# One scan per unit over all 128 rows, with small transfers for the fourth pair of heads

## The chip, the cores and the metric

The kernel runs on one core of one Trainium2 chip. The metric is the device time of one execution in microseconds. The kernel before takes 502.21 us (median of three runs, 501.99 to 503.38). A profiled execution of its own gives the rows that are quoted here; a line number such as L550 is a line of the kernel before.

## The reference

A linear attention with a decaying state is followed by a two-layer network with a piecewise gate. There are 4 batches, 8 heads, 768 steps and 48 channels per head, all in float32:

```
state = zeros(B, H, D, D)
for t in range(S):
    cur    = outer(u * k[t], v[t])
    y[t]   = r[t] @ (state + cur)
    state  = w[t][:, None] * state + outer(k[t], v[t])
x = y as (B*S, 384)
h = x @ w_in                                  # 384 -> 2048
g = h where h >= 1, 0 where h <= -1, else (h + 1)**2 / 4
out = g @ w_out                               # 2048 -> 384
```

w lies between 0.8 and 0.95, so products of w over 64 steps stay within float32.

## The kernel before, in words

**Units and blocks.** Time is cut into 12 units (0 to 11) of 64 steps for all 4 batches, 256 tokens each (`UT`). Two units make one block of 512 tokens; the network works on 6 blocks. For each block and each of 16 slices f of the hidden layer there is a step: nine products in (L1348), the gate on ScalarE and VectorE, nine products out (L1368). The last three blocks are "fast": their products out are combined in a scheme with fewer multiplications (L1042), for which sums of weight parts are built first (L964, `sums_of`). Each 32-bit number is carried as a high and a low part of the reduced type fp32r.

**One attention unit** (`attention(u, ...)`). Channels stand in the rows: a head has 48 channels and takes 64 rows, 16 of them padding, so two heads fill 128 rows and the 8 heads make 4 pairs. Two pairs are one half q, so w comes as two tiles of 520 columns (2 pairs x 4 batches x 65) and r and k as two tiles of 2 x 512. VectorE scans each half forward (L550: running products of w, called p) and backward (L545, called y), multiplies k by y (L571) and r by p (L621). The last p of each chunk is the chunk's total decay; ScalarE copies it to `ptot`. Then TensorE does:

- `among` (L591), 64 small products of scaled k with scaled r, whose lower triangle VectorE picks into `r_` (L597);
- `ktrans` (L630), transposes of k; `umat` (L660), k by v, the addition to the state;
- `cross` and `along` (L703), r with the old state and the picked matrix with v.

VectorE adds to the state and multiplies it by the total decay (`step` L678, `fade` L681, reading `ptot`). ScalarE and VectorE bring the result into the block's x, and six small transfers per unit put the result's fourth pair from the tile `last` into the 16 padding rows of the three other pairs (`fill`, L827). From unit 6 on, ScalarE checks w against 1 on the loaded tile (`guard`, L846 and L847); w of the units before is loaded again for this in the fast stage. Units 0 to 2 (`early`) get the term with u by a second `among`; later units get it from POOL and VectorE on the natural layout `nk`. Units 0 and 1 are `alone`: their x gets the fourth pair through TensorE (L800).

**Buffers.** w and r/k have three tiles for halves each, so one and a half units fit. In the fast stage the attention's tiles are used again: the gate's results lie in r/k tiles 0 to 2, and the sums of weights are built in the p tile (`part`).

**The order of the work.** `Plan` takes each operation with its engine, an assumed cost, what it reads and writes, and a due time, and simulates the engines. Each engine takes the ready operation with the smallest key. The result is one fixed order per engine, written out by hand, and semaphores keep the engines together. The first keys come from due times (`LEADS`, `group`); then 40 rounds draw new keys from the latest possible times plus noise from `SEED`, and the order with the earliest simulated end is kept. For a transfer it takes 0.63 or 0.45 us on SP's queue, then bytes at 390 KB per us plus 2.0 us, and 0.15 us until the reader can go; at most eight are in flight. Where TensorE would be idle early on, products of zeros are filled in (L439). If a check finds w or the running products out of bounds, a general kernel runs afterwards; it is not touched by the change.

Of the kernel before, what the change touches and what calls it, by code (L numbers as in the profile page):

```python
# [23 lines left out]
UT = 256  # L24
# [5 lines left out]
SEG = 2 * NC * (C + 1)  # L30
HP = 64
# [17 lines left out]
SCRATCH = 2048  # L49
# [9 lines left out]
BACK, SHAKES, SHAKE, SEED = 4, 40, 0.7, 1  # L59
# [278 lines left out]

GUARDED = 6
# [17 lines left out]
def attention_moe(tc, a):  # L357
# [24 lines left out]
    seeds = one([128, 2 * NC, C + 1], F32, "seeds")  # L382
# [4 lines left out]
    wq = tiles(3, [128, SEG + 1], F32, "wq")  # L387
    rk = tiles(3, [128, 2, 512], F32, "rk")
# [3 lines left out]
    p_ = one([128, 4 * NC, C + 1], F32, "p")  # L392
    y_ = one([128, SEG], F32, "y")
# [29 lines left out]
    for t, v, name in ((zero, 0.0, "zero"), (seeds, 0.0, "seeds"), (minus_one, -1.0, "minus_one")):  # L423
        op("POOL", 0.5, SOON, (), [name], lambda t=t, v=v: G.memset(t, v))
# [79 lines left out]

    def attention(u, when, lead=None):
# [12 lines left out]
        slot = [(2 * u + 1 - q) % 3 for q in range(2)]  # L518
        pv = p_.rearrange("p (q n) c -> p q n c", q=2)
# [6 lines left out]
        for q in (1, 0):  # L526
            load(due, wq[slot[q]], a["w"][u, q], [("w", slot[q])], first=rank(1 - q))
            load(due, rk[slot[q]], a["rk"][u, q], [("k", slot[q]), ("r", slot[q])], first=rank(4 - 2 * q))
# [10 lines left out]
        sv = seeds.rearrange("p n c -> p (n c)")  # L539

        def scan(q, back):
            w = wq[slot[q]]
            if back:
                V.reciprocal(seeds[:, :, C], pv[:, q, :, C])
                V.tensor_tensor_scan(  # L545
                    out=y_[:, ::-1], data0=w[:, SEG:0:-1], data1=sv[:, ::-1], initial=0.0, op0=ALU.mult, op1=ALU.add
                )
            else:
                V.memset(seeds[:, :, C], 0.0)
                V.tensor_tensor_scan(  # L550
                    out=pv[:, q].rearrange("p n c -> p (n c)"), data0=w[:, 0:SEG], data1=sv, initial=0.0,
                    op0=ALU.mult, op1=ALU.add,
                )

        def parts(q, i):
            return rk[slot[q]][:, i].rearrange("p (n c) -> p n c", c=C)

        def with_u(q):
            for pr in range(2):
                cs = slice(pr * UT, pr * UT + UT)  # L560
                A.mul(ku[:, q, cs], rk[slot[q]][:, 1, cs], u_col[:, 2 * q + pr : 2 * q + pr + 1])

        for q in (1, 0):
            s = slot[q]
            if early:
                op("ACT", 1.0, due, [("k", s), "cst"], [("ku", q), "nk"], lambda q=q: with_u(q))
            op("DVE", 1.3, due, [("w", s)], [("p", q), "seeds"], lambda q=q: scan(q, False), port=True)
            op("ACT", 0.2, due, [("p", q)], [("ptot", u, q)], lambda q=q: A.copy(
                ptot[:, 16 * u + 8 * q : 16 * u + 8 * q + 8], pv[:, q, :, C]))
            op("DVE", 1.45, due, [("w", s), ("p", q)], ["y", "seeds"], lambda q=q: scan(q, True), port=True)  # L570
            op("DVE", 0.69, due, ["y"], [("k", s)], lambda q=q: V.tensor_tensor(  # L571
                out=parts(q, 1), in0=parts(q, 1), in1=y_.rearrange("p (n c) -> p n c", c=C + 1)[:, :, 1:], op=ALU.mult), port=True)

        def tokens(q, i, pr, c2, g=None):
            lo = pr * UT + c2 * 128 + (0 if g is None else g * C)
            return slice(lo, lo + (128 if g is None else C))


        dv = d_.rearrange("p c (a h) -> p h a c", h=2)

        def among(to, left):

            for pair in range(4):
                q, pr = divmod(pair, 2)
                for c2 in range(2):
                    for g in range(2):
                        for h in range(2):
                            i = slice(HP * h, HP * h + HP)
                            cs = tokens(q, 0, pr, c2, g)
                            lo = (pair * 2 + c2) * C  # L590
                            PE.matmul(  # L591
                                bank[to[h]][HP * g : HP * g + C, lo : lo + C], lhsT=left(q)[i, cs],
                                rhs=rk[slot[q]][i, 0, cs], start=True, stop=True,
                            )
# [6 lines left out]
        both = [("r", slot[0]), ("r", slot[1])]  # L601
        if early:
            bd = [take(), take()]
            op("PE", 1.27, due, [("ku", 0), ("ku", 1), "nk", *both], [("b", bd[0]), ("b", bd[1])],
               lambda: among(bd, lambda q: ku[:, q]), code=128)
# [14 lines left out]
        for q in (1, 0):  # L620
            op("DVE", 0.69, due, [("p", q)], [("r", slot[q])], lambda q=q: V.tensor_tensor(  # L621
                out=parts(q, 0), in0=parts(q, 0), in1=pv[:, q, :, 0:C], op=ALU.mult), port=True)
# [3 lines left out]
        def ktrans(q, b):  # L626
            for pr in range(2):
                for c2 in range(2):
                    lo = (pr * 2 + c2) * 128
                    PE.transpose(out=bank[b][:, lo : lo + 128], in_=rk[slot[q]][:, 1, tokens(q, 1, pr, c2)], identity=ident)  # L630

        op("PE", 1.27, due, [("k", slot[0]), ("k", slot[1]), *both], [("b", ba[0]), ("b", ba[1])],
# [805 lines left out]
```

## Time and profile before

| what | value |
|---|---|
| profiled execution | 502.04 us, span 500.5 us |
| median of three runs | 502.21 us |
| TensorE (PE) busy | 486.8 us, 97% |
| VectorE (DVE) busy | 402.8 us, 80% |
| ScalarE (ACT) busy | 314.3 us, 63% |
| GpSimd (POOL) busy | 102.5 us, 20% |
| moved by DMA | 54.3 MB, mean 108 GB/s |
| granted TensorE clock | 0.992 |

The span is the time from the first to the last instruction; the execution's own time is 1.5 us longer. A share of busy time is a mean over stages with different limits, so the table alone does not say what bounds the kernel. In a timeline row the columns are start, length, engine, line, operation, tiles and count, all times in us. In a group's row there are count, busy time, mean length in ns, the engine's idle time just before, and what ended that idle time.

### The profile page before, as it was taken

How to read it: one execution, taken by the hardware profiler on the slowest of the kernel's cores; microseconds unless marked ns; L12 is line 12 of the kernel's file. 1: busy time of each engine (PE TensorE's matmuls, PEld its weight loads, DVE VectorE, ACT ScalarE, POOL GpSimd, SP SyncE). 2: the span in 40 equal slices, each digit the busy share in tenths (PEclk: the TensorE clock that was granted, in tenths of full speed). 3: DMA queues.
4: the chain of work that ended last, by engine and by line, in shares of the span. 5: the costliest groups of instructions: out<-in, count | busy, mean ns of one | idle time of the engine just before them, and what ended most of it. 6: DMA issues, size and time to landing. Idle time of an engine off the chain costs nothing.

```text
span 500.5 us, 13728 instructions
## 1 busy us (share of the span) xinstructions
PE 486.8 (97%) x5767; PEld 426.3 (85%) x5767; DVE 402.8 (80%) x702; ACT 314.3 (63%) x658; POOL 102.5 (20%) x80
## 2 busy tenths in 40 slices
PE   6989999999999999999999999999999999999994
PEld 4679988889999998887878878889898989899884
DVE  6999999997787898898979988787877575675563
ACT  4769988936455566655645746778876565465451
POOL 1745515403111121112032132432200000000000
PEclk9989999999999999999999999999999999999998
DMA  8987641424242434436256012122241000100002
GB/s 316 357 331 265 251 151 64 138 45 155 74 155 85 140 124 134 160 121 225 44 203 201 11 53 85 31 62 44 42 107 22 0 2 1 53 12 0 3 1 69
DMA packets 33286, 54.30 MB, mean 108 GB/s; under 512 B 15424, under 2 KB 22720, under 8 KB 33216
## 3 DMA queue, kind: packets, MB, share of 16 engines
q1 hardware_dynamic: 32784, 52.95, 31.8%
q8 instruction: 47, 0.77, 0.7%
q10 hardware_dynamic: 432, 0.39, 0.2%
q14 instruction: 23, 0.19, 0.1%
HBM read 47.04 MB, written 4.72 MB: 103 GB/s over the span
## 4 chain that ended last, share of the span: by engine, by line
PE 92%; DVE 4%; issue 2%; DMA 1%; ACT 1%; SPq 0%; DVEq 0%; ACTq 0%
PE h L1348 41%; PE acc L1368 21%; PE acc L1042 10%; PE bank L1042 9%; PE bank L703 4%; PE bank L591 3%; PE bank L630 2%; PE bank L660 1%; DVE fl L487 1%; DMA cst<-in_consts 1%; DVE y L545 1%; DVE r L597 0%; DVE rk L571 0%; PE h L660 0%; DVE wt L490 0%
## 5 line engine op out<-in xcount | busy, mean ns | idle before, releaser
L1348 PE MATMUL h<-x,wt 128*128 128x512 f32 (+1 forms) x1035 | 221.4, 362 | 2.2 <-DVE x L779 1.4
L1348 PEld LDWEIGHTS h<-x,wt 128*128 128x128 f32 x1035 | 169.7, 190 | 30.9 <-DVE x L779 1.6
L1368 PE MATMUL acc<-gh,wt 128*128 128x256 f32 (+1 forms) x402 | 80.0, 334 | 0.0
L1368 PEld LDWEIGHTS acc<-gh,wt 128*128 128x128 f32 x402 | 61.3, 188 | 7.8
L1004 DVE SCALAR_TENSOR_TENSOR rk<-rk,h 128x512 f32<-128x512 f32 x48 | 32.8, 684 | 36.3 <-ACT rk L1003 36.0
L1157 ACT ACTIVATE g<-h 128x256 f32<-128x256 f32 (+1 forms) x67 | 31.8, 475 | 46.5 <-PE h L1348 41.4
L1001 ACT ACTIVATE rk<-h 128x512 f32<-128x512 f32 x48 | 28.7, 597 | 42.8 <-PE h L1348 42.7
L485 POOL TENSOR_SCALAR wraw<-fl 128x768 uint16<-128x768 f32 x13 | 41.5, 3195 | 47.2 <-ACT wraw L483 46.2
L1159 DVE SCALAR_TENSOR_TENSOR g<-g,h 128x256 f32<-128x256 f32 (+1 forms) x67 | 35.2, 528 | 12.6 <-ACT g L1158 11.2
L1368 PE MATMUL acc<-gl,wt 128*128 128x256 f32 (+1 forms) x201 | 44.5, 329 | 0.0
L1161 ACT CAST gh<-g 128x256 fp32r<-128x256 f32 (+1 forms) x67 | 32.9, 498 | 13.4 <-DVE g L1159 7.9
L617 POOL TENSOR_TENSOR r<-cst,d 128x512 f32<-128x512 f32 x18 | 21.6, 1222 | 90.2 <-PE bank L703 46.8
L1162 DVE TENSOR_TENSOR gl<-g,gh 128x256 fp32r<-128x256 f32 (+1 forms) x67 | 39.0, 591 | 1.0 <-ACT gh L1161 0.6
L1368 PEld LDWEIGHTS acc<-gl,wt 128*128 128x128 f32 x201 | 32.4, 188 | 4.0
L1158 ACT ACTIVATE g<-g 128x256 f32<-128x256 f32 (+1 forms) x67 | 33.9, 511 | 1.0
L550 DVE TENSOR_TENSOR_SCAN p<-wq,seeds 128x520 f32<-128x520 f32 x24 | 30.8, 1284 | 3.1 <-DMA wq<-in_w 2.2
L609 POOL TENSOR_TENSOR nk<-nk 128x768 f32<-128x768 f32 x9 | 17.4, 1933 | 71.8 <-DMA nk<-in_nk 49.4
L545 DVE TENSOR_TENSOR_SCAN y<-wq,seeds 128x520 f32<-128x520 f32 x24 | 30.4, 1266 | 0.8
L1003 ACT ACTIVATE rk<-rk 128x512 f32<-128x512 f32 x48 | 30.4, 633 | 0.9
L1010 DVE TENSOR_TENSOR gl<-rk,gh 128x512 fp32r<-128x512 f32 x36 | 25.8, 720 | 4.1 <-ACT gh L1009 3.9
L1010 DVE TENSOR_TENSOR g_again<-rk,nk_again 128x512 fp32r<-128x512 f32 x33 | 23.3, 710 | 6.8 <-ACT nk_again L1009 6.5
L1009 ACT CAST gh<-rk 128x512 fp32r<-128x512 f32 x36 | 22.1, 616 | 8.3 <-DVE rk L1004 5.7
(214 smaller groups left out, 910.8 us busy)
## 6 DMA issues: line engine op xcount, KB each, us to landing
rk<-in_rk SPq DMA_DIRECT2D x24, 512.0 KB, 5.4
wraw<-in_wbits SPq DMA_DIRECT2D x16, 768.0 KB, 6.9
nk<-in_nk SPq DMA_DIRECT2D x9, 768.0 KB, 5.6
wq<-in_w SPq DMA_DIRECT2D x24, 260.5 KB, 3.4
vn<-in_v SPq DMA_DIRECT2D x12, 384.0 KB, 7.0
last<-in_w SPq DMA_DIRECT2D x12, 256.0 KB, 2.9
out_y<-xf SPq DMA_DIRECT2D x15, 128.0 KB, 1.8
out_y<-g SPq DMA_DIRECT2D x6, 256.0 KB, 2.2
```

The costliest lines, as they stand in the source:

```text
L485: op(on, 0.62 if f in SIGNS else 3.2, due, [("fl", k)], [("raw", f)], lambda: e.tensor_scalar(out=half(1), in0=s, scalar1=0.0, scalar2=327 ...
L545: V.tensor_tensor_scan(out=y_[:, ::-1], data0=w[:, SEG:0:-1], data1=sv[:, ::-1], initial=0.0, op0=ALU.mult, op1=ALU.add)
L1004: op("DVE", 0.66, due, [("h", n)], [qk], lambda: V.scalar_tensor_tensor(out=gf, in0=gf, scalar=1.0, in1=bank[plan.given[hk]], op0=ALU.min, ...
L1010: op("DVE", 0.67, due, [key, ("h", i, k)], fresh_in(("l", i, k)), lambda: V.tensor_tensor(out=spare(k, 3 + i), in0=x, in1=spare(k, i).bitc ...
L1042: PE.matmul(bank[i][:, half * UT : half * UT + UT], lhsT=w[wi], rhs=g[gi], start=(b, i) not in opened, stop=True, skip_group_check=True)
L1157: op("ACT", c, due, [("h", n)], [("g", gk)], lambda: nc.scalar.activation(gs, hs(), AF.Relu, scale=0.5, bias=0.5), uses=[hk])
L1158: op("ACT", c, due, (), [("g", gk)], lambda: nc.scalar.activation(gs, gs, AF.Square))
L1159: op("DVE", 0.13 + 0.53 * k, due, [("h", n)], [("g", gk)], lambda: nc.vector.scalar_tensor_tensor(out=gs, in0=gs, scalar=1.0, in1=hs(), op ...
L1161: op("ACT", c, due, [("g", gk)], [("gh", gk)], lambda: nc.scalar.copy(ghs, gs))
L1162: op("DVE", 0.17 + 0.54 * k, due, [("g", gk), ("gh", gk)], [("gl", gk)], lambda: nc.vector.tensor_tensor(out=gls, in0=gs, in1=ghs.bitcast( ...
L1348: nc.tensor.matmul(hp, lhsT=wx[f][:, cs], rhs=xt[:, j, :], start=n == 0, stop=n == 8)
L1368: nc.tensor.matmul(o[j], lhsT=wx[f][:, cs], rhs=gt, start=first and i == 0, stop=stop and i == 2, skip_group_check=True)
```

## The change

**Dense rows.** From unit 2 on (the third unit), w, r and k come in a dense layout of three slots of 4 x 64 steps: slots are the pairs 0, 1 and 2 in their own rows, and the 48 channels of pair 3's two heads lie in the 16 padding rows of each half, a third in each slot. One forward and one backward scan over 780 columns (`LONG`) replace two of 520; one product with y and one with p do for the unit. Then `gather` sends pair 3's scaled k, and in the same way r, to the rows of its own: six transfers of 16 KB each for k and six for r, from tile to tile, issued by SP.

**In place.** In units 3 to 11 r is multiplied by p before the backward scan, which then writes over p. Unit 2 writes y into the tile `xf[0]`, takes pair 3 of the unscaled k and r from two extra loads (for its product with u), and gathers over them.

**Padded units.** Units 0 and 1 keep two halves. Their w and scans lie in `xf`, and r and k are loaded separately.

**The total decay.** r gets a 65th column of ones per chunk, so its product with p leaves the total there; `fade` and `step` read it instead of `ptot`. `ptot` is still copied for the check, and `ptot` and `above` are filled by POOL first, as not all their columns are written.

**TensorE.** `among` and `inter` read 48 rows per head instead of 64.

**Buffers.** w: two tiles for whole units. r and k: two tiles for whole units. `y` is gone and p is smaller. In the fast stage the gate's results lie in the first 1024 columns of both r/k tiles, differences in the last 1024 columns of the first, and the sums of weights are built in the last 1024 columns of the second. The guard runs once per unit over 780 columns. `SCRATCH` is 1024 instead of 2048 and `SEED` 8 instead of 1.

```diff
-SCRATCH = 2048
+SCRATCH = 1024
-BACK, SHAKES, SHAKE, SEED = 4, 40, 0.7, 1
+BACK, SHAKES, SHAKE, SEED = 4, 40, 0.7, 8
+PADDED = {0, 1}
...
-    wq = tiles(3, [128, SEG + 1], F32, "wq")
-    rk = tiles(3, [128, 2, 512], F32, "rk")
+    wd = one([128, 2, LONG + 1], F32, "wd")
+    rk = tiles(2, [128, 4 * NC * (C + 1) + 4 * UT], F32, "rk")
...
+        if padded:
+            for q in (1, 0):
+                load(due, flat_of(xf[0])[:, q * (SEG + 1) : (q + 1) * (SEG + 1)], a["w"][u, q], [("xw", q)], first=rank(1 - q))
+                load(due, rt_[:, 2 * q : 2 * q + 2]..., a["rq"][u, q], keys("r", 2 * q, 2 * q + 1), first=rank(4 - 2 * q))
+                load(due, kd_[:, 2 * q : 2 * q + 2]..., a["kq"][u, q], keys("k", 2 * q, 2 * q + 1), first=rank(4 - 2 * q))
+        else:
+            load(due, wd[:, buf], a["wd"][u], [("w", buf)])
+            load(due, kd_[:, 0:3].rearrange("p a t -> p (a t)"), a["kd"][u], keys("k", 0, 1, 2))
+            load(due, rt_[:, 0:3].rearrange("p a n c -> p (a n c)"), a["rd"][u], keys("r", 0, 1, 2))
...
+        def gather(of, t, size):
+            for j in range(3):
+                for h in range(2):
+                    lo = HP * h
+                    op("SP", 0.63, due, [(of, buf, j)], [(of, buf, 3, j, h)], lambda t=t, j=j, lo=lo: nc.sync.dma_start(
+                        out=t[lo + 16 * j : lo + 16 * j + 16, 3], in_=t[lo + D : lo + HP, j]), size=16 * 4 * size)
...
+            op("DVE", cp, due, [wk], [pk, "seeds"], lambda w=w, p=p, n=n: scan(w, p, None, n), port=True)
+            if in_place:
+                scaled_r(pairs, p, pk, cr)
+                gather("r", rt_.rearrange("p a n c -> p a (n c)"), NC * (C + 1))
+            op("DVE", cy, due, [wk, pk], [yk, "seeds"] + ..., lambda w=w, p=p, y=y, n=n: scan(w, p, y, n), port=True)
+            op("DVE", ck, due, [yk], keys("k", *pairs), lambda pairs=pairs, y=y: times_y(pairs, y), port=True)
+            if not padded:
+                gather("k", kd_, UT)
...
-            return ptot[:, 16 * u : 16 * u + 16].rearrange("p (a c g) -> p c g a", c=2, g=2)[:, :, g]...
+            return rt_.rearrange("p a (c g) t -> p c g a t", g=2)[:, :, g, :, C]...
...
-        for q in range(2):
-            if u >= GUARDED:
-                guard(wq[slot[q]][:, 0:SEG], ("w", slot[q]), 2 * u + q, (when, 0.0))
+        if u >= GUARDED:
+            guard(wd[:, buf, 0:LONG], ("w", buf), 2 * u, (when, 0.0), 1.5)
...
-    quad = [quads(mem(("q", k), flat(rk[k], 0, 1024), ("k", k), ("r", k))) for k in range(2)]
-    diff = quads(mem("t", flat(rk[2], 0, 1024), ("k", 2), ("r", 2)))
+    quad = [quads(mem(("q", k), rk[k][:, 0:1024], *rk_keys[k])) for k in range(2)]
+    diff = quads(mem("t", rk[0][:, 1024:2048], *rk_keys[0]))
...
-    part = flat(p_, 0, 1024)
-    mem("a", None, ("p", 0), ("p", 1))
+    part = rk[1][:, 1024:2048]
+    mem("a", None, *rk_keys[1])
```

More of the change, by code (lines that the diff above doesn't have):

```diff
@@ L422, in attention_moe @@
     SOON = 0, 200.0
-    for t, v, name in ((zero, 0.0, "zero"), (seeds, 0.0, "seeds"), (minus_one, -1.0, "minus_one")):
+    for t, v, name in ((zero, 0.0, "zero"), (seeds, 0.0, "seeds"), (minus_one, -1.0, "minus_one"), (ptot, 1.0, "ptot"), (above, 0.0, "above")):
         op("POOL", 0.5, SOON, (), [name], lambda t=t, v=v: G.memset(t, v))
@@ L516, in vs, with keys @@
             return v[i, c2, head * D : head * D + n]
-        slot = [(2 * u + 1 - q) % 3 for q in range(2)]
-        pv = p_.rearrange("p (q n) c -> p q n c", q=2)
+        buf = u % 2
+        padded = u in PADDED
+        in_place = not early
+        rt_, kd_ = rt[buf], kd[buf]
+        late_key = [(j, h) for j in range(3) for h in range(2)]
+        def keys(of, *pairs):
+            out = []
+            for pair in pairs or range(4):
+                out += [(of, buf, pair)] if pair < 3 else [(of, buf, 3, *x) for x in late_key]
+            return out
+        rkeys, kkeys = keys("r"), keys("k")
         ku = nk.rearrange("p a b c -> p (a b c)")[:, 0:1024].rearrange("p (q c) -> p q c", q=2)
@@ L555, in parts @@
-        def parts(q, i):
-            return rk[slot[q]][:, i].rearrange("p (n c) -> p n c", c=C)
-        def with_u(q):
[L559 to L572, printed above, removed]
@@ new lines, in attention, with scaled_r @@
+        if early:
+            for q in (1, 0):
+                op("ACT", 1.0, due, [*keys("k", 2 * q, 2 * q + 1), "cst"], [("ku", q), "nk"], lambda q=q: with_u(q))
+        def scaled_r(pairs, p, pk, cost):
+            op("DVE", cost, due, [pk], keys("r", *pairs), lambda: times_p(pairs, p), port=True)
+        for q, pairs, w, wk, p, pk, y, yk, (cp, cy, ck, cr) in todo:
+            n = len(pairs) * NC
+            op("DVE", cp, due, [wk], [pk, "seeds"], lambda w=w, p=p, n=n: scan(w, p, None, n), port=True)
+            lo = 16 * u + 8 * q
+            op("ACT", 0.2, due, [pk], [("ptot", u, q), "ptot"], lambda p=p, n=n, lo=lo: A.copy(ptot[:, lo : lo + n], by_chunk(p, n)[:, :, C]))
+            if in_place:
+                scaled_r(pairs, p, pk, cr)
+                gather("r", rt_.rearrange("p a n c -> p a (n c)"), NC * (C + 1))
+            op("DVE", cy, due, [wk, pk], [yk, "seeds"] + ([("xw", 1)] if not padded and not in_place else []), lambda w=w, p=p, y=y, n=n: scan(w, p, y, n), port=True)
+            op("DVE", ck, due, [yk], keys("k", *pairs), lambda pairs=pairs, y=y: times_y(pairs, y), port=True)
+            if not padded:
+                gather("k", kd_, UT)
@@ L619, in attention @@
                     in1=dv[:, h].unsqueeze(3).broadcast_to([128, 4, 2, C]), op=ALU.mult), port=True)
-        for q in (1, 0):
-            op("DVE", 0.69, due, [("p", q)], [("r", slot[q])], lambda q=q: V.tensor_tensor(
-                out=parts(q, 0), in0=parts(q, 0), in1=pv[:, q, :, 0:C], op=ALU.mult), port=True)
+        if not in_place:
+            for _, pairs, _, _, p, pk, _, _, costs in todo:
+                scaled_r(pairs, p, pk, costs[3])
+            if not padded:
+                gather("r", rt_.rearrange("p a n c -> p a (n c)"), NC * (C + 1))
         ba = [take(), take()]
@@ L1216, in attention_moe @@
             products(n)
-    every = [("ptot", u, q) for u in range(NU) for q in range(2)] + [("above", n) for n in range(2 * NU)]
+    every = ["ptot", "above"] + [("ptot", u, q) for u in range(NU) for q in range(2)] + [("above", n) for n in range(2 * NU)]
     op("DVE", 1.0, (len(steps) - 12, 0.0), (), [*every, "ok"], check)
```

126 lines of the change are left out of this document (76 added, 50 removed).

## The prediction

> **What bounds the kernel now.** I read the busy time in stages first, because a mean over the whole run mixes a start, a long middle and an end with different limits. Columns: stage, its length, then busy time and count for PE, weight loads, DVE, ACT and POOL, then granted clock, DMA share and GB/s.
>
> ```profile
> 0.00:40.00 40.00, 33.23 (x672) 26.00 (x675) 34.06 (x50) 25.28 (x47) 20.31 (x20) 0.96 0.84 314
> 40.00:60.00 20.00, 19.63 (x260) 19.26 (x251) 19.07 (x35) 18.76 (x44) 9.43 (x4) 1.00 0.74 268
> 60.00:300.00 240.00, 239.72 (x3506) 206.59 (x3505) 213.16 (x367) 145.86 (x332) 54.40 (x33) 1.00 0.37 124
> 300.00:484.00 184.00, 184.00 (x1270) 164.84 (x1270) 129.42 (x240) 120.44 (x231) 18.39 (x24) 1.00 0.13 32
> 484.00:500.50 16.50, 10.19 (x78) 9.57 (x76) 7.05 (x14) 3.99 (x7) 0.00 (x0) 0.87 0.17 53
> ```
>
> From 60 to 484 us TensorE is busy 423.72 of 424 us at the full granted clock. VectorE is at 89% (213.16 of 240) in the stage that holds most attention units and at 70% in the one after. So VectorE is busy there without being the limit. Only the first 40 us (DMA at 0.84, DVE at 34 of 40) and the last 16 us leave TensorE short of work, and part of its 33.23 us in the start is filler on the zero tile. The list of TensorE's waits says the same; its first rows are:
>
> ```profile
> PE h L445 <- POOL zero L424: 2.8, 1, 2.8
> PE h L1348 <- DVE x L779: 1.4, 1, 1.4
> ```
>
> 2.8 us is the wait for the first memset, and no group of later waits reaches 1.5 us. Nothing that VectorE does after 60 us is waited for in a way that could be won back.
>
> **What is removed: VectorE work.** These groups (instructions, busy us, mean ns) are the work whose shape changes. 24 scans of each kind are 12 units with two halves each.
>
> ```profile
> L550 DVE TENSOR_TENSOR_SCAN p<-wq,seeds 128x520 f32<-128x520 f32 x24 | 30.8, 1284 | 3.1 <-DMA wq<-in_w 2.2
> L545 DVE TENSOR_TENSOR_SCAN y<-wq,seeds 128x520 f32<-128x520 f32 x24 | 30.4, 1266 | 0.8
> L621 DVE TENSOR_TENSOR rk<-rk,p 128x512 f32<-128x512 f32 x24 | 17.3, 726 | 0.0
> L571 DVE TENSOR_TENSOR rk<-rk,y 128x512 f32<-128x512 f32 x24 | 16.7, 697 | 4.9 <-DMA rk<-in_rk 4.8
> L847 ACT ACTIVATE wq<-wq,minus_one 128x520 f32<-128x520 f32 x12 | 8.8, 732 | 0.2
> L846 ACT ACTIVATE wq<-wq 128x520 f32<-128x520 f32 x12 | 7.7, 639 | 6.6 <-DVE y L545 6.6
> ```
>
> A dense unit scans 780 columns once instead of 520 twice. In proportion to columns the forward scan is 1.284 x 780/520 = 1.93 us instead of 2.57, the backward one 1.90 instead of 2.53, the product with k (768 columns) 1.05 instead of 1.39, and the product with r (780) 1.11 instead of 1.45. That is 0.64 + 0.63 + 0.34 + 0.34 = 2.0 us per unit, 20 us over the ten dense units (2 to 11, counted from 0). ScalarE's guards save 2 x (0.732 + 0.639) - 1.5 x (0.732 + 0.639) = 0.69 us in each of six units. For units 3 to 11 all of this lies beside a full TensorE, since unit 3's first scan is this one:
>
> ```profile
> 75.77 1.24 DVE L550 TENSOR_TENSOR_SCAN p<-wq,seeds 128x520 f32<-128x520 f32 x1
> ```
>
> Priced at zero, with a gain of at most the 0.28 us that TensorE is short of 240 as the other end. Loaded bytes fall too (two w of 260.5 KB and two rk of 512 KB become 390, 384 and 390 KB; unit 2 adds 258 KB), where the DMA share is 0.37: zero again. The TensorE products keep count and columns, but 48 instead of 64 rows go in. The nearest rows are products of the same 64 columns with 48 and with 64 on the other side of the tile:
>
> ```profile
> L703 PE MATMUL bank<-r,vn 64*48 64x64 f32 x128 | 2.2, 217 | 0.0
> L703 PE MATMUL bank<-r,vn 64*64 64x64 f32 x640 | 11.1, 218 | 0.0
> ```
>
> One nanosecond apart: zero, with both ends there. VectorE's fade now reads the total beside r, in the same shape: zero.
>
> **The start.** Only unit 2's dense work can touch the part where TensorE is not full. In VectorE's timeline its forward scan stands right ahead of a weight's decode, and the chain that ended last runs through that decode.
>
> ```profile
> 36.84 1.24 DVE L550 TENSOR_TENSOR_SCAN p<-wq,seeds 128x520 f32<-128x520 f32 x1
> 38.00 1.51 DVE L487 SCALAR_TENSOR_TENSOR fl<-fl,wraw 128x768 int32<-128x768 int32 x1
> ```
>
> If the new order moves the scan behind the decode, 1.24 us is gained; if it stays as one 1.86 us scan, 0.62 us is lost. I take the middle, **-0.3 us**.
>
> Units 0 and 1 keep their padded halves, but r and k come as two transfers per half. SP's issues take 0.43 us each, and two more stand ahead of the first weight (first row; the others are used below):
>
> ```profile
> 3.31 0.43 SPq L469 DMA_DIRECT2D wraw<-in_wbits  x1
> 8.31 0.33 SPq L419 DMA_DIRECT2D rk<-in_rk  x1
> 18.48 0.33 SPq L419 DMA_DIRECT2D wq<-in_w  x1
> 18.91 1.95 SPq L419 DMA_DIRECT2D rk<-in_rk  x2
> ```
>
> Ends 0 and +0.9 us; I take 0, since the bytes ahead of it are the same and the DMA engines are 84% busy over these 40 us, so the weight waits for bytes and not for its issue. Unit 1's w must now wait in SP's order until unit 0 has scanned (its two staging places are single). In the chain, unit 0's last scan and unit 1's first one are
>
> ```profile
> 8.94 1.25 DVE y L545
> 15.49 1.25 DVE p L550
> ```
>
> so that wait ends 5.3 us (15.49 - 10.19) before the data is used. The two memsets of ptot and above join POOL's first ones; they read zero because the filler needs only the zero tile.
>
> **What is added: 12 small transfers per unit.** The scaled r and k of the fourth pair go back to their own rows, six SP issues of 16 KB each, and the first `among` of scaled k waits for the last. The nearest thing in the trace is the spread of `last` into x: the same partition-to-partition kind, six at a time, 16 or 32 KB (KB, then median us to landing), and over all 60 of them the least, median and most:
>
> ```profile
> x<-last SPq DMA_DIRECT2D x36, 32.0 KB, 2.9
> xf<-last SPq DMA_DIRECT2D x24, 16.0 KB, 3.5
> DMA to landing us min/median/max: 1.7/2.9/6.6
> ```
>
> The planner writes one fixed order per engine. For such a transfer it reckons 2.04 us from issue to landing and 0.15 us for the signal: 2.19 us. The time that the plan knows costs nothing, since it starts the unit earlier and fills TensorE with products meanwhile. What it does not know is 2.9 - 2.19 = 0.71 us, or 3.5 - 2.19 = 1.31 us by the 16 KB row. TensorE stops for that only if the plan put `among` closer than this behind its last input, because its queue is in order and every product behind it waits too. How close it puts them now: VectorE's last product of a unit, and the `among` in the chain that ended last.
>
> ```profile
> 171.85 0.68 DVE L621 TENSOR_TENSOR rk<-rk,p 128x512 f32<-128x512 f32 x1
> 255.25 0.68 DVE L621 TENSOR_TENSOR rk<-rk,p 128x512 f32<-128x512 f32 x1
> 272.53 1.55 DVE L621 TENSOR_TENSOR rk<-rk,p 128x512 f32<-128x512 f32 x1
> 294.77 0.68 DVE L621 TENSOR_TENSOR rk<-rk,p 128x512 f32<-128x512 f32 x1
> ```
>
> ```profile
> 173.50 1.09 PE bank L591 x64
> 255.98 1.16 PE bank L591 x64
> 274.72 1.09 PE bank L591 x64
> 296.73 1.09 PE bank L591 x64
> ```
>
> The distances are 0.97, 0.05, 0.64 and 1.28 us for units 5, 9, 10 and 11. At 0.71 us late the stops are 0.66 + 0.07 = 0.7 us; at 1.31 us they are 0.34 + 1.26 + 0.67 + 0.03 = 2.3 us; units not listed count as zero. I take **+0.7 us**, by the median of all 60, with 0 and +2.3 us as ends. Behind the waiting issues on SP stand the next loads; with two whole buffers for w, r and k now, they have a unit's time to spare (18.7 and 22.0 us between the last three rows above).
>
> The Trainium skill speaks against such transfers: "DMA: Bandwidth & Descriptors", section Rules for kernel authors, says to coalesce, since under 64 KB one mostly pays overhead; its section Anatomy of one DMA puts that overhead at about 2.0 us. The spread's 2.9 us median is longer than that page's figure; by 2.0 us the plan would be right, no stop would follow, and the sum would be 0.7 us lower.
>
> **Sum.** The profiled run is 502.04 us (span 500.5). 502.04 - 0.3 + 0.7 = 502.4; the median of the runs is 0.17 us above the profiled one, so 502.6 us.
>
> **Rivals.** (1) Late transfers decide, slower. Place: the `among` of scaled k in units 2 to 11. It decides once a transfer lands over 2.19 us plus the unit's distance after its issue. At the 16 KB row's 3.5 us that is +2.3 us over the units listed: 502.21 + 2.3 = 504.5; at longer landings (6.6 us occurs) up to 507. For it: distances as small as 0.05 us. Against: the plan may keep more distance now that the buffers are double.
>
> (2) The fast stage's sums start late, slower. They were written over p, which was free once VectorE had multiplied r in the last unit; now they share the last unit's r and k buffer, which TensorE reads until the end of `along`.
>
> ```profile
> 295.97 0.75 DVE L964 TENSOR_TENSOR p<-wt 128x256 f32<-128x256 f32 x2
> 299.79 0.68 DVE L964 TENSOR_TENSOR wq_again<-p,wq_again 128x512 fp32r<-128x512 f32 x1
> ```
>
> ```profile
> 303.03 1.56 PE bank L703 x96
> ```
>
> ```profile
> 308.00 0.30 PEld L1042 LDWEIGHTS bank<-gh,wq_again 128*128 128x128 f32 x2
> ```
>
> Now the first sums take 295.97 to 300.47, 4.5 us. If they wait for 304.59 they end at 309.1, against the first product that uses them, at 308.00: 1.1 us late, and the later pairs follow through the same buffer, so 502.21 + 1.1 = 503.3 us, and up to twice or three times that, 505. Against: `rk<-in_rk` is what VectorE waits for in L571 (4.8 us); with two whole buffers the last unit can load and run earlier.
>
> (3) The start becomes shorter, faster. SP stood until 18.48 us for a w slot and issued unit 1's second r and k behind it at 18.91 us; the new buffer is free from the beginning, so it can be issued beside the first ones, at 8.31. If that and the lighter unit 2 take away four tenths of the 6.77 us (40 - 33.23) in which TensorE stood idle in the start, 2.7 us by this estimate, the time is 502.2 - 2.7 = 499.5. Against: the DMA engines were busy anyway, and the first product waited for unit 0's x (1.4 us above), not for unit 1.
>
> The plan's seed changes too, so the whole order is drawn anew. That adds spread of either sign that no row prices.
>
> **How the numbers follow.** My forecast 0.38, rivals 0.23, 0.08 and 0.31. About 0.3% (1.5 us) is what a measurement of this kernel tells from no change. The forecast lies inside it, so same 0.38; rivals 1 and 2 give slower 0.31; rival 3 gives faster 0.31. Around 502.21, the terms' lower ends give 502.21 - 1.24 - 0.28 = 500.7 and their upper ends 502.21 + 0.62 + 0.9 + 2.3 = 506.0, the forecast's own range. With rival 3, rival 1 beyond its row and the spread of the new order, the range is 498.7 to 506.5 us.
>
> **What would show it.** Right: scans of 780 columns at 1.9 us, TensorE still full from 60 to 484 us, a TensorE wait on L591 or L630 for a DMA of about 1 us in all. Wrong upward: such waits of 2 us or more in total, or a gap in TensorE at the start of the fast stage. Wrong downward: the stage 0 to 40 us holds more products and less filler. If the scan's time did not follow its columns, the VectorE figures are wrong, but not the time.

## The result, and the profile after

The changed kernel takes 508.14 us (median of 4 runs, 506.37 to 509.55); the kernel before took 502.70 beside it (4 runs). The ratio is 1.0105, 95% interval [1.0076, 1.0135]. A second series gave 508.60 us and 1.0102 [1.0065, 1.0139]. The change makes the kernel about 1% slower, 1.6 us beyond the upper end of the predicted range. The profiled execution of after is one of 507.15 us with a span of 505.6 us.

VectorE did what was forecast. The groups of the profile after (count, busy us, mean ns, idle time ahead):

```profile
L580 DVE TENSOR_TENSOR_SCAN p<-wd,seeds 128x780 f32<-128x780 f32 x10 | 19.1, 1913 | 0.4
L583 DVE TENSOR_TENSOR_SCAN p<-wd,seeds 128x780 f32<-128x780 f32 x9 | 16.0, 1783 | 0.4
...
L598 DVE TENSOR_TENSOR rk<-rk,p 128x780 f32<-128x780 f32 x10 | 10.2, 1015 | 3.2 <-DMA rk<-in_rd 3.2
L593 DVE TENSOR_TENSOR rk<-rk,p 128x768 f32<-128x768 f32 x9 | 8.6, 951 | 0.0
```

The windows of after, by the same edges as before:

```profile
0.00:40.00 40.00, 33.41 (x692) 25.54 (x696) 33.85 (x51) 23.93 (x45) 18.83 (x21) 1.00 0.87 319
40.00:60.00 20.00, 19.85 (x243) 18.93 (x233) 19.05 (x30) 18.37 (x42) 10.66 (x3) 1.00 0.40 133
60.00:300.00 240.00, 238.16 (x3601) 205.38 (x3600) 195.06 (x309) 138.38 (x310) 57.73 (x38) 1.00 0.39 128
300.00:484.00 184.00, 184.00 (x1143) 164.52 (x1143) 128.30 (x236) 119.24 (x225) 15.97 (x20) 1.00 0.12 31
```

From 60 to 300 us VectorE fell from 213.16 to 195.06 us, and TensorE stayed full but for 1.84 us. So the added time hardly shows as idle time. It shows as more busy time for the same work: the first rows of the two pages, before and then after, have the same 5767 TensorE instructions and 4.0 us between them.

```profile
PE 486.8 (97%) x5767; PEld 426.3 (85%) x5767; DVE 402.8 (80%) x702; ACT 314.3 (63%) x658; POOL 102.5 (20%) x80
```

```profile
PE 490.8 (97%) x5767; PEld 428.5 (85%) x5767; DVE 385.9 (76%) x642; ACT 306.9 (61%) x630; POOL 103.2 (20%) x82
```

A stop of a tenth of a microsecond between two overlapping small products counts as busy, so such a loss must be looked for in the lengths of groups. In the chain that ended last (start, length, engine, tile, line, count), `among` took 1.09 us in nearly every unit before. After:

```profile
83.96 1.57 issue
...
152.28 1.09 PE bank L645 x64
...
171.95 1.33 PE bank L645 x64
...
193.96 1.33 PE bank L645 x64
...
212.52 1.38 PE bank L645 x64
...
228.98 1.38 PE bank L645 x64
```

Of these only unit 4 (152.28) is at the old length; the other four are about a quarter of a microsecond longer. The first row is a gap in the middle of unit 2's `along` in which TensorE waits for nothing that this view shows (more on it at the end). TensorE's waits name no transfer as the cause of a stop in `among`:

```profile
PE h L449 <- POOL zero L428: 3.2, 1, 3.2
PE bank L758 <- issue: 1.6, 1, 1.6
PE bank L685 <- DVE rk L593: 1.2, 2, 0.8
PE h L1401 <- DVE x L832: 0.9, 1, 0.9
PE bank L853 <- DMA nk<-in_perm: 0.6, 1, 0.6
```

And the small transfers are not late (KB each, then median us from issue to landing):

```profile
rk<-rk SPq DMA_DIRECT2D x60, 16.2 KB, 1.8
rk<-rk SPq DMA_DIRECT2D x60, 16.0 KB, 2.1
```

These are medians; the longest of the 120 took 4.8 us. Even so, in this trace the last of a unit's twelve transfers had landed 2.3 us or more before the 49th product of `among`, the first one of the fourth pair, in nine of the ten dense units. In unit 11 it had landed 0.03 us before it, and that `among` is no longer than unit 5's.

**Where the 5.1 us went.** I added up, over all TensorE products of the two profiled executions, the distance from one start to the next less a fixed length for its shape (233.3 ns for 512 columns, 116.7 for 256, 109 for the transposes, 17 for the small ones; filler on the zero tile counts as lost, and so do the time before the first product and the time after the last). What is left over is time that TensorE lost:

| stage or kind | before, us | after, us | difference |
|---|---|---|---|
| 0 to 60 us | 25.4 | 24.8 | -0.6 |
| 60 to 300: `among` | 0.04 | 1.94 | +1.9 |
| 60 to 300: products of 256 columns | 2.58 | 4.24 | +1.7 |
| 60 to 300: `cross` and `along`, with the gap of 1.57 | -0.91 | 0.95 | +1.9 |
| 60 to 300: all others | 3.1 | 3.3 | +0.2 |
| after 300 us | 8.27 | 8.33 | +0.1 |
| all | 38.5 | 43.6 | +5.1 |

Three suspects follow from this table: the waits on the small transfers, a dearer 256-column product, and the order of the work. The layout gives the second a cause to test: with the changed tiles, x, the gate's results, the state, the picked matrix `r_` and the transposed k stand 64 bytes further on, modulo 512.

### The profile page after: what moved, and what is told of

Its sections match the earlier page's. It is cut to its first block, busy times and chain, and to the rows that moved or that the text cites. A ratio compares the mean times of both kernels' runs of the same rounds, so it can differ in the third digit from the quotient of the medians.

```text
span 505.6 us, 13831 instructions
## 1 busy us (share of the span) xinstructions
PE 490.8 (97%) x5767; PEld 428.5 (85%) x5767; DVE 385.9 (76%) x642; ACT 306.9 (61%) x630; POOL 103.2 (20%) x82
## 4 chain that ended last, share of the span: by engine, by line
PE 90%; DMA 4%; DVE 2%; issue 1%; ACT 1%; SPq 1%; DVEq 0%
PE h L1401 40%; PE acc L1421 20%; PE acc L1095 10%; PE bank L1095 9%; PE bank L758 4%; PE bank L645 3%; DMA wraw<-in_wbits 2%; PE bank L685 2%; DMA rk<-in_rq 1%; PE bank L715 1%; DMA out_y<-g 1%; SPq L423 1%; DVE fl L491 0%; PE bank L443 0%; PE h L715 0%
## 5 line engine op out<-in xcount | busy, mean ns | idle before, releaser
L489 POOL TENSOR_SCALAR wraw<-fl 128x768 uint16<-128x768 f32 x13 | 43.3, 3345 | 44.5 <-ACT wraw L487 32.9
L1215 DVE TENSOR_TENSOR gl<-g,gh 128x256 fp32r<-128x256 f32 (+1 forms) x67 | 40.6, 618 | 2.3 <-ACT gh L1214 2.2
L1063 DVE TENSOR_TENSOR gl<-rk,gh 128x512 fp32r<-128x512 f32 x36 | 24.2, 685 | 2.7 <-ACT gh L1062 2.6
L1062 ACT CAST nk_again<-rk 128x512 fp32r<-128x512 f32 x33 | 20.4, 617 | 9.5 <-DVE rk L1057 6.9
L651 DVE COPY_PREDICATED r<-below,bank 128x512 f32<-128x512 int32 x23 | 16.1, 731 | 5.0 <-PE bank L645 4.9
```

What stands on the lines that cost most here:

```text
L489: op(on, 0.62 if f in SIGNS else 3.2, due, [("fl", k)], [("raw", f)], lambda: e.tensor_scalar(out=half(1), in0=s, scalar1=0.0, scalar2=327 ...
L1062: op("ACT", 0.6, due, [key], fresh_in(("h", i, k)), lambda: A.copy(spare(k, i), x))
L1063: op("DVE", 0.67, due, [key, ("h", i, k)], fresh_in(("l", i, k)), lambda: V.tensor_tensor(out=spare(k, 3 + i), in0=x, in1=spare(k, i).bitc ...
L1215: op("DVE", 0.17 + 0.54 * k, due, [("g", gk), ("gh", gk)], [("gl", gk)], lambda: nc.vector.tensor_tensor(out=gls, in0=gs, in1=ghs.bitcast( ...
```

## The experiments

All were run beside the kernel before, five rounds each.

**Are the transfers, their issues or the reads of them what costs?** Two kernels keep the changed kernel's order of work. One sends the transfers where nobody reads them, the other drops them; both leave out the fourth pair's transferred rows.

```diff
-                        out=t[lo + 16 * j : lo + 16 * j + 16, 3], in_=t[lo + D : lo + HP, j])
+                        out=away[u, 0 if of == "r" else 1, j, lo // HP, :, 0 : size], in_=t[lo + D : lo + HP, j])
```

> The changed kernel with its 12 transfers per dense unit kept, at the same places of SP's order and of the same size, but sent to a spare place in HBM that nothing reads, so that TensorE has no transfer to wait for at the fourth pair. What it leaves out: the fourth pair's scaled k and r do not arrive in units 2 to 11, so the fourth pair's results are wrong. Theory A (each of these waits is paid as an instruction on TensorE's in-order queue although the transfers have long landed; the trace of the changed kernel shows L645 at 1.33 to 1.38 us per unit in place of 1.09): L645 goes back to 1.09 us and the time falls by 2 us (8 units by 0.25) against 508.1, to about 506. Theory B (addresses of x and of the gate's tiles) and theory C (the newly drawn order): no change, 507 to 509.

```diff
-                    op("SP", 0.63, due, ..., lambda t=t, j=j, lo=lo: nc.sync.dma_start(...), size=16 * 4 * size)
+                    op("SP", 0.63, due, ..., lambda t=t, j=j, lo=lo: None, size=16 * 4 * size)
```

> The changed kernel in the same planned order without its 12 transfers per dense unit. It leaves them out, so the fourth pair's results are wrong in units 2 to 11. Theory A: the same as with the transfers sent elsewhere, about 506; if it is lower than that one by over 1 us, the transfers themselves cost time (SP's issues, the DMA engines) beyond the waits. Theories B and C: 507 to 509.

Measured: 503.96 us (ratio 1.0027 [1.0001, 1.0053]) with the transfers unread, and 504.24 us (1.0038 [1.0017, 1.0058]) without them. They do not differ from each other, so 120 transfers and their issues on SP cost nothing that can be measured. Reading them costs 4 us, twice what I had expected from the longer `among` alone. The group of `among`'s products of scaled k with scaled r, in the changed kernel and then with the transfers unread:

```profile
L645 PE MATMUL bank<-rk 48*64 48x64 f32 x736 | 16.4, 223 | 0.0
```

```profile
L647 PE MATMUL bank<-rk 48*64 48x64 f32 x736 | 14.6, 221 | 0.3 <-issue 0.3
```

1.8 us of busy time goes with the reads, although the mean of one product hardly moves: a busy sum counts the stops between overlapping products, a mean does not.

**Does the address cost?** In the changed kernel the tile d, 64 bytes, is allocated last, which puts the tiles behind it back to the address of before, modulo 512; in the kernel before, a gap of 64 bytes is put in front of them.

```diff
-    d_ = one([128, 2, H], F32, "d")
     ...
     xf = tiles(len(FLAT), [128, 3, WIDE], F32, "xf")
+    d_ = one([128, 2, H], F32, "d")
```

> The changed kernel with one 64 byte tile (d) allocated last, so that r, kt, st, x and the gate's tiles lie 64 bytes lower, at the same address modulo 512 as in the kernel before. Theory B (a product of 256 columns takes 120 ns in place of 116.7 because of the address of its operands; some 700 of them in blocks 0 and 1): they go back to 117 ns and the time falls by 2.3 us, to about 505.8. Theories A and C: no change, 507 to 509, products of 256 columns stay at 119 to 120 ns.

```diff
     d_ = one([128, 2, H], F32, "d")
+    gap = one([128, 16], F32, "gap")
```

> The kernel before with a 64 byte gap ahead of r, kt, st, x and the gate's tiles, so that they lie at the address modulo 512 that they have in the changed kernel. Theory B: products of 256 columns go from 116.7 to 120 ns and the time rises by 2.3 us to about 505. Theories A and C: no change, 502 to 503.4.

Measured: 507.83 us (1.0116 [1.0075, 1.0157]) with the address of before, no gain that the median shows; 504.30 us (1.0046 [1.0018, 1.0073]) for the kernel before with the gap, a loss of 1.5 us. One of the groups of 256 columns shows the step in both directions: before, before with the gap, after, after with the old address.

```profile
L1368 PE MATMUL acc<-gl,wt 128*128 128x256 f32 x114 | 19.5, 279 | 0.0
```

```profile
L1369 PE MATMUL acc<-gl,wt 128*128 128x256 f32 x114 | 19.8, 282 | 0.0
```

```profile
L1421 PE MATMUL acc<-gl,wt 128*128 128x256 f32 x114 | 19.8, 282 | 0.0
```

```profile
L1421 PE MATMUL acc<-gl,wt 128*128 128x256 f32 x114 | 19.5, 279 | 0.0
```

3 ns each; the first blocks have 342 products in and 228 + 114 out of this width. The effect is there both ways; in the changed kernel's median the other losses cover it.

**The changed kernel again, and both causes out.** The first is the changed kernel itself. The second sends the transfers away and puts d last; it leaves out the same rows as the first experiment.

> The changed kernel once more, unaltered, beside the next three. Its first times lay between 506.4 and 509.6 us. If the transfers land late in some executions only (theory L), the times spread again over 2 us or more and the median stays 506.5 to 509. If the cost is a fixed one per wait (theory W, TensorE's queue takes time for each semaphore of a transfer), the times lie within 1 us of each other and near the profiled 507.15.

> Nobody reads the fourth pair's transferred rows (they go to a spare place in DRAM, so the fourth pair's products of units 2 to 11 are computed from other rows), and x, g, gh, gl, r and k^T stand at the addresses of before, modulo 512 bytes. If the two causes add up (waits on the transfers, and 64 bytes of address), 504.0 - 1.5 = 502.5 us, no different from before. If the address costs nothing of its own, 504.0 us as without it. If the order of the work itself is worse, over 503.5 us.

Measured: 508.60 us (505.77 to 509.91) for the changed kernel; 503.13 us against 503.30 of before with both out, ratio 1.0000 [0.9977, 1.0022]. With the reads of the transfers and the addresses taken out, the medians show nothing that is left of the loss. (The transfers unread alone left 1.0027; the intervals overlap, so the part of the address in it is not settled by these two.) That the account closes is not shown, though, because the executions differ in granted clock. The six of the kernel before at a mean granted clock of 0.996 or more took 500.86 to 502.55 us, median 501.5; the ten of the kernel with both out took 501.35 to 503.93, median 503.05. At a like clock some 1.6 us are left, which may be the order's. The profiled executions show where the clocks differ: from 28.5 to 31.9 us it is 0.51 in the kernel before, and 1.00 in the changed one. The widths say nothing on late landing, against what I expected of them, because the kernel before itself ranged over 5 us in its 29 runs (500.86 to 506.39), largely with the clock. The profiled run of this series took 509.91 us, longer than the median, and it has a wait that could be a cause (first VectorE's for the load of r, then TensorE's for g):

```profile
DVE rk L598 <- DMA rk<-in_rd: 11.2, 5, 3.5
...
PE h L1401 <- DVE g L1212: 1.3, 1, 1.3
```

VectorE's wait is 3.2 us in all in the profile of 507.15 us (the row of L598 above). In place, r is multiplied before the backward scan, so a late load holds all of VectorE's queue. That is tested below.

**A plan that leaves the transfers more time.** An addition `more=3.0` to the planned end of each small transfer, and the old addresses.

```diff
-                end[n] = bus + 2.0
+                end[n] = bus + 2.0 + op["more"]
```

> The changed kernel with the addresses of before, and a planner that reckons 5.04 instead of 2.04 us for each of these small transfers, so that the products that read them stand some 3 us later in TensorE's order. The waits stay. Theory L (they land late): the stops go, 503 to 504 us, and the spread between executions falls below 1 us. Theory W (each wait costs TensorE time although the data is there): no better than the same kernel without the added 3 us, 505 to 508 us.

Measured: 506.49 us (1.0065 [1.0040, 1.0090]). That is within what the theory of dear waits allows and above what late landing would leave, though the order was drawn anew, and its part in this is not known. Its `among` is as long as ever:

```profile
170.82 1.33 PE bank L645 x64
...
212.40 1.33 PE bank L645 x64
```

So 3 us more in the plan between the transfer and its reader do not shorten the reader. What `among` loses is not waiting for data.

**Fewer transfers, same bytes.** The host lays out the dense rows so that row 48 + p, slot j holds channel 3p + j. Then 16 rows of three slots are, in the order of memory, the 48 rows of the fourth pair, and one transfer does for three. The addresses are again the old ones.

```diff
-            for j in range(3):
-                for h in range(2):
...
-                        out=t[lo + 16 * j : lo + 16 * j + 16, 3], in_=t[lo + D : lo + HP, j]), size=16 * 4 * size)
+            for h in range(2):
...
+                    out=t[lo : lo + D, 3], in_=t[lo + D : lo + HP, 0:3]), size=48 * 4 * size)
```

> The changed kernel with the addresses of before, and each fourth pair's rows brought by two transfers of 48 KB instead of six of 16 KB (the dense rows are laid out on the host so that one block of memory order serves; same bytes): four waits per unit on TensorE instead of twelve, and the order is planned anew with fewer issues. Theory W: two thirds of the waits' cost of 3 to 4 us goes, 504 to 505 us. Theory L: a transfer of 48 KB lands no earlier than one of 16 KB, so 505 to 508 us.

Measured: 505.09 us (1.0037 [1.0014, 1.0060]). `among` is at 1.09 to 1.12 us from unit 2 on; two rows of the chain:

```profile
192.50 1.12 PE bank L644 x64
...
213.16 1.12 PE bank L644 x64
```

The transfers' landing:

```profile
rk<-rk SPq DMA_DIRECT2D x20, 48.8 KB, 2.2
rk<-rk SPq DMA_DIRECT2D x20, 48.0 KB, 3.0
```

The bigger transfers land later than the small ones, and `among` is shorter and the kernel faster: the number of transfers that TensorE waits for counts, not their landing. (The order is drawn anew here too, so the 3 us of the whole kernel are not the transfers' alone.)

**Only half of the transfers read.** Same order as the changed kernel; of r and k, one tensor's six go to the spare place, and its rows of the fourth pair are left out.

```diff
+                        out=away[u, 0, j, lo // HP, :, 0 : size] if of == "r" else t[lo + 16 * j : lo + 16 * j + 16, 3], ...
```

> The changed kernel, same order; only r's six transfers per unit go to a spare place in DRAM (the fourth pair's r rows of units 2 to 11 are left out), k's six stay. In the built program the first two products of the fourth pair then wait for 3 and 3 transfers instead of 4 to 5 and 4. In the trace of the changed kernel `among` took 1.09 us with one such wait, 1.11 with 3 and 3, 1.23 with 3 and 4, 1.33 to 1.38 with 4 to 5 and 4. Theory Q3 (only a fourth and later wait on one instruction costs TensorE time): 1.11 us each and the whole loss of the waits gone, 503.5 to 504.5 us. Theory Q (each wait costs the same): 1.2 us each and half of the loss of 4.5 us left, 506 us. Theory L (k's transfers land late, as they are issued last): no gain, 508 us.

> The other half: k's six transfers go to the spare place (the fourth pair's k rows of units 2 to 11 are left out), r's six stay, same order. 3 and 3 waits again. Theory Q3: 503.5 to 504.5 us. Theory Q: 506 us. Theory L: r's transfers are issued a scan earlier than k's and can't be late, so 504 us here and 508 us with k's.

Measured: 505.10 us (1.0043 [1.0024, 1.0061]) with k's read, 506.37 us (1.0062 [1.0041, 1.0082]) with r's read. In the chain of the first:

```profile
169.82 1.12 PE bank L647 x64
...
191.60 1.11 PE bank L647 x64
...
209.95 1.11 PE bank L647 x64
```

Here the count of waits explains `among` to the hundredth. The program names, with each instruction, what it waits for. Unit 5's first two products of the fourth pair, in the changed kernel and with k's transfers alone:

```
after     among, product 49: waits for transfer queues 4, 3, 6, 1, 0
          among, product 50: waits for transfer queues 5, 7, 4, 2
k's only  among, product 49: waits for transfer queues 6, 3, 1
          among, product 50: waits for transfer queues 5, 4, 2
```

In the trace one of these waits goes with the product, and the others stand before it as instructions of their own, which hold up to two waits each. The trace has them on TensorE's sequencer. Start in us, length in ns, the semaphores they wait for, in the changed kernel and with k's alone:

```
after     172.377 51 S105, S104     172.488 51 S109, S101
          172.614 51 S107           172.720 51 S110, S105
k's only  170.246 51 S109, S104     170.371 51 S107, S105
```

Counted from 60 us on in the traces of the two kernels and all the experiments, the usual time from the first to the last start of `among` follows their number (a few single ones lie elsewhere):

| extra wait instructions in one `among` | first to last start, us |
|---|---|
| 0 | 0.94 |
| 2 | 0.97 |
| 3 | 1.08 |
| 4 | 1.19 |
| 5 | 1.29 |

One ahead of each of two products is all but hidden; each further one adds 0.11 us. In the profile after, the ten dense units are together 1.9 us longer than ten of 0.94, the 1.9 of the account above. The Trainium skill has the first half of this ("Perfetto Trace Analysis", section Identifying Dependency Chains): instructions that wait for several engines may get semaphore instructions put before them. The trace agrees, here for waits on several transfer queues; the price, 0.11 us, is this case's.

What I had expected of the times was only half met. By the count of waits both kernels should have come to 504; they are 1.1 and 2.4 us above the kernel that reads none. What the two differ by goes along with the clock: the median of the mean granted clock is 0.998 with k's read and 0.9935 with r's, and the three executions with r's at 0.996 or 0.997 took 504.2 to 504.9 us. In the second's profiled execution, which took 509.37 us, the gap in `along` was 2.9 us, and from 86.4 to 93.2 us the granted clock was 0.50:

```profile
PE bank L760 <- issue: 2.9, 1, 2.9
```

**Is the late load of r the rest?** 3 us more reckoned for that load: in the changed kernel, and with two transfers per tensor.

```diff
-            load(due, rt_[:, 0:3].rearrange("p a n c -> p (a n c)"), a["rd"][u], keys("r", 0, 1, 2))
+            load(due, rt_[:, 0:3].rearrange("p a n c -> p (a n c)"), a["rd"][u], keys("r", 0, 1, 2), more=3.0)
```

> The changed kernel; the planner reckons 3 us more for the load of a dense unit's r, so that it is issued earlier or its first use stands later in VectorE's order. Twelve transfers and TensorE's waits on them stay. Theory R (in the slower executions the load of r lands late, VectorE stands for it up to 3.5 us at a time and TensorE then stops for g): VectorE's wait for that load falls from 3.2 to 11.2 us to under 2 us and the time to 505 to 506.5 us. Theory Q (only the waits on the small transfers in TensorE's queue cost): 506.5 to 509 us as before.

> Two transfers of 48 KB per tensor instead of six of 16 KB, the addresses of before, and 3 us more reckoned for the load of r. With two transfers alone the time was 505.09 us against 503.3 before. Theory R: 1 to 2 us less than with the two transfers alone, so 503 to 504 us. Theory Q: no change, about 505 us.

Measured: 509.37 us (1.0132 [1.0102, 1.0162]) and 503.97 us (1.0030 [1.0009, 1.0052]; without it 1.0037). The wait did shrink in the first,

```profile
DVE rk L598 <- DMA rk<-in_rd: 1.6, 1, 1.6
```

and the time did not. The second time lies in the range that I had given the theory, but its ratio is not told apart from that without the 3 us. Nothing here supports the theory of the late load.

**How much is the order?** The change draws the order anew. The changed kernel with the seed of before, two transfers per tensor with seed 35, and the kernel before with two other seeds:

```diff
-BACK, SHAKES, SHAKE, SEED = 4, 40, 0.7, 8
+BACK, SHAKES, SHAKE, SEED = 4, 40, 0.7, 1
```

> The changed kernel with the seed of the kernel before (1 in place of 8): the same work and transfers in another order. If the loss belongs to the change, 506 to 509 us, as with seed 8. If it belongs to this one order, near 503 us.

> Two transfers of 48 KB per tensor and the addresses of before, in the order that another seed draws (35). If what is left of the loss with two transfers (505.09 against 503.3 us) is a matter of this order, 502 to 504 us, or below the kernel before. If it belongs to the transfers, about 505 us.

> The kernel before with seed 11, whose planned end is the earliest of eleven draws. The changed kernel moved from 508.6 to 512.9 us when its seed alone was changed. If the order alone moves the kernel before as much, this lies 2 us or more from 502.9, and may be as fast as the two-transfer versions at 501.6 to 502.2. If the order matters less without the small transfers, within 1.5 us of 502.9.

> The kernel before with the seed of the changed kernel (8). Same question: 2 us or more from 502.9 if the order alone moves the time, within 1.5 us if not.

Measured: 512.94 us (1.0190 [1.0155, 1.0224]) for the changed kernel with seed 1; 504.36 us (1.0040 [1.0019, 1.0061]) with two transfers and seed 35; 503.49 us (1.0014 [0.9983, 1.0045]) and 504.17 us (1.0021 [0.9996, 1.0046]) for the kernel before. The order moves the kernel before by about 1 us and the changed one by 4. Most of that lies in the start. By the account above, TensorE lost 28.4 us of the first 40 with seed 1 and 23.3 with seed 8, which is 5.1 of the 6.6 us between the spans of their profiled executions, and the granted clock there was 0.83 instead of 1.00. In this slowest one the small transfers land even earlier,

```profile
rk<-rk SPq DMA_DIRECT2D x60, 16.2 KB, 1.8
rk<-rk SPq DMA_DIRECT2D x60, 16.0 KB, 1.8
```

and `among` takes 1.44 us where it has five extra wait instructions:

```profile
255.88 1.44 PE bank L645 x64
...
274.49 1.44 PE bank L645 x64
```

**A version that beats both.** Two transfers per tensor, the old addresses, the 3 us for r's load, and the two seeds of forty whose planned end is earliest.

```diff
-BACK, SHAKES, SHAKE, SEED = 4, 40, 0.7, 8
+BACK, SHAKES, SHAKE, SEED = 4, 40, 0.7, 23
```

> Two transfers of 48 KB per tensor, the addresses of before, 3 us more reckoned for the load of r, seed 5: the order with the earliest planned end of forty draws. The same with seed 8 took 503.97 us against 502.91. If the order decides what is left, 502 us or less; if not, 504 us.

> The same with seed 23, the second earliest planned end. Together with seeds 8 and 5 it shows how far the order alone moves the time: within 1 us of each other if it is not the order, and one of them below 502.5 us if it is.

Measured: 502.19 us (0.9976 [0.9957, 0.9995]) with seed 5 and 501.63 us (0.9972 [0.9949, 0.9996]) with seed 23, against 502.75 of the kernel before. Both intervals lie below 1: a gain of a quarter of a per cent. In seed 23's chain `among` is at 1.09 to 1.12 us and no gap is listed in `along`. From 100 to 300 us TensorE is full, and VectorE has 40 us to spare:

```profile
100.00:300.00 200.00, 200.00 (x3203) 173.96 (x3202) 159.28 (x266) 106.91 (x253) 39.51 (x32) 1.00 0.38 114
```

So the dense scans, once their transfers are few, do no harm and bring little. Whether they or the choice of the order bring it is not separated: the best of eleven planned orders of the kernel before (seed 11) was no faster, but forty were not drawn for it.

## Why the prediction was wrong, point by point

- **VectorE's saving is worth nothing: right.** 402.8 - 385.9 = 16.9 us less work (20 forecast for the dense units alone; scans of 1.91 and 1.78 us for the forecast 1.93 and 1.90), beside a TensorE that stayed full. Of the guard, the bytes and the 48 rows nothing shows in the account either; none of them was tested alone.
- **The start, -0.3 us: right in sign.** The loss from 0 to 40 us fell by 1.24 us, the lower end of that step, and 40 to 60 gave 0.7 back. The scan did move behind decodes (it starts at 41.06 us instead of 36.84), but the gain can't be put down to that: the kernel before had half the clock for 3.4 us there and the changed one had not, so the sign may be luck. The two further issues of SP do not show. Of rival 3 a little came true, without effect on the end.
- **Twelve small transfers, +0.7 us: this is the step that failed.** I priced them only as landing later than the plan reckons, from 2.9 us of a bigger, busier transfer. They landed in 1.8 and 2.1 us by the median, near the 2.04 planned, and ahead of their readers, and by that reckoning cost nothing. But each of them is also a semaphore that TensorE's queue must test, four or five ahead of one product, and the nearest row (1.09 us with one or two such waits) could not show what five cost. The reads of the transferred rows cost 4 to 4.6 us (508.14 and 508.60 against 503.96): 1.9 of it are the wait instructions themselves, by their count. Rival 1 had the place and nearly the size (504.5 to 507 us), but late landing is not the mechanism: the transfers landed before they were read, a reader planned 3 us later stayed as long, and bigger transfers that land later made it shorter.
- **No term for addresses.** The list of tiles in the diff moves everything behind them by 64 bytes, and I did not add up the sizes. Measured on the kernel before it is +1.5 us, on the changed kernel with the transfers unread 504.0 against 503.1, in two series whose intervals overlap.
- **"The order is drawn anew, spread of either sign that no row prices": too lightly said.** Two seeds of the changed kernel are 4.3 us apart, more than any term of the sum, most of it in the start; three of the kernel before lie within 1.1 us of each other by their ratios.
- **Rival 2, late sums in the fast stage: did not happen.** TensorE is full from 300 to 484 us.
- **What I said would show it did not.** I looked for a listed wait of TensorE on a transfer; none is listed. The loss stands in the busy time of `among` (16.4 against 14.6 us).

What stays open: the reads cost 4 to 4.6 us by the medians, the wait instructions 1.9 us by the trace. Half of the reads leave 1.1 to 2.4 us, part of it the clock's, though `among` is then as a rule no more than 0.03 us longer. The gap in `along` of unit 2 is not the rest: with the transfers unread it is 1.8 us, without them 1.2, against 1.6 in the changed kernel.

What that gap is can be read from the traces, if not proved. The page of each run lists a queue of 47 packets of 16 KB that carry instructions (q8). Up to 484 us the twenty traces together have 21 stops of TensorE, of 0.2 to 2.9 us, that the profile puts to "issue". Every one of them ends 1.25 to 1.51 us after such a packet has ended; of the 15 stops from 60 us on that it puts to another engine, one does. In the changed kernel the packet ran from 83.27 to 84.20 us, and TensorE went on at 85.53. So these stops look like waits for instructions that were loaded late. They are in other orders and places too (2.2 us with seed 1, 1.0 us in unit 10's `among` in the execution of 509.91 us), so they also make executions of one program differ. No experiment moved such a load, so the cause is argued from the times alone.

## What to carry to other kernels

Count, for each instruction of the engine that sets the end, how many different transfers it waits for: up to three cost next to nothing here, and every further one or two were an instruction of their own in its queue, at 0.11 us. Three short transfers into one operand are better laid out so that one transfer does for them, and a change that resizes tiles should keep the addresses of those behind them. When an engine is full before and after and yet the time grows, compare busy sums of equal groups, not lists of waits.

## What the runs showed of the hardware

- Wait instructions on TensorE's sequencer have records of 51 ns each; two behind one another ahead of a product delay it, 0.11 us for each beyond the first.
- 64 bytes of address make a product of 256 columns 3 ns longer by the group's mean (279 to 282 ns), both ways; from start to start it is 117.0 to 117.4 ns against 119.7 to 120.1. Products of 512 columns stayed at 233.0 to 233.5 ns from start to start.
- A transfer of 16 KB from rows to rows of the same tile landed in 1.8 to 2.1 us, one of 48 KB in 2.2 to 3.0. The Trainium skill, "DMA: Bandwidth & Descriptors", section Anatomy of one DMA, has about 2.0 us as the fixed part on the path issued from GpSimd; these are issued by SP, and the small ones come near that figure. Its rule to coalesce transfers under 64 KB (section Rules for kernel authors) gave the right sign in this case, on the reader's side: three in one took `among` from 1.33 to 1.11 us, while the 120 small ones that nobody read cost nothing measurable.
- All 21 stops of TensorE up to 484 us that no semaphore explains, in twenty traces, ended 1.25 to 1.51 us after a packet of 16 KB of instructions had ended.
- In the kernel before, the granted clock was 0.51 from 28.5 to 31.9 us, and its executions at a mean granted clock of 0.996 or more were about 1.8 us shorter than its median (501.5 against 503.3 us in one series).
